# Windowed attention in front of a mixture of experts: scores of each chunk of queries with its own keys only, and a softmax that reads the banks

## The chip, the cores and the metric

One core of one Trainium2 chip. The time is that of one execution on the device, in microseconds (us). PE is TensorE, DVE VectorE, ACT ScalarE, POOL GpSimd, and SP the queue that issues all the DMAs. A "bank" is a part of PSUM, the memory that TensorE writes; the other tiles lie in SBUF.

## The reference

Attention over chunks of 32 queries: a chunk sees 16 keys to its left, its own 32 and 8 to its right (fewer at the ends of the sequence), and 8 memory keys, 64 in all. There are 4 batches, 8 heads, 768 positions and a head size of 64. The result goes through 4 experts, each weighted by a probability of the token.

```python
for c in range(nc):                        # 24 chunks of 32
    q_c = q[:, :, c_start:c_end]
    k_full = np.concatenate([mem_k, k[:, :, l_start:r_end]], axis=2)
    v_full = np.concatenate([mem_v, v[:, :, l_start:r_end]], axis=2)
    scores = scale * np.matmul(q_c, k_full.transpose(0, 1, 3, 2))
    scores = scores - np.max(scores, axis=-1, keepdims=True)
    a = np.exp(scores)
    a = a / (np.sum(a, axis=-1, keepdims=True) + 1e-09)
    out[:, :, c_start:c_end] = np.matmul(a, v_full)
...
for e in range(E):                         # x: 3072 x 512
    h = np.maximum(x @ w1[e], 0.0)         # 512 x 1024
    out += p[:, e:e + 1] * (h @ w2[e])     # 1024 x 512
```

## The kernel before

The work of the attention is cut into 32 units of 96 queries, three chunks (`UQ` = 96, `NCU` = 3): eight units a batch, four batches. A unit has a window of 128 keys, the 120 that its three chunks see and the 8 memory keys put in at column 56 (`MEM`). TensorE multiplies all 96 queries with all 128 keys, head by head. The heads go in pairs: head size 64 fills half of TensorE's rows, and the two heads of a pair (`j` = 0, 1) lie in the two halves. Their scores go to the two banks of one tile (`s_ps`, or `att_ps` in the head).

Of each row of 128 scores a chunk needs 64 (`KW`). `PIECES` says which: 0 to 64 for the first chunk, 32 to 96 for the second, and for the third the memory's 8 at column 56 and 56 from column 72. Four copies for a unit bring them into `s_sb` (96 x 8 x 64, a `spot` in the head for most units), where keys outside of the sequence are filled with a very low number. Maximum, exponential, sum and division run on `s_sb`. Four more copies spread the result over `band` (96 x 8 x 128), which is zero elsewhere, and `band` is turned into `aT` (128 keys by 96 queries): in seven 32x32 block transposes on VectorE in the steady part, on TensorE in the head. TensorE multiplies `aT` with the values into `x_ps`. The attention's output is the experts' input `x`.

There are three stages. In the **head**, `early_scores`, `early_turn` and `early_mix` work on the eight units of the first batch (S, T and X in the text `FIRST_BLOCK`), among them products of the first expert (M, N) and products of zeros (W). In the steady part the experts of one batch run while `window` works on the next batch's units: nine calls of it for a batch, each of which scores one unit and then mixes the unit before. The experts' products make up nearly all of TensorE's work.

The order on TensorE is that in which the program adds its steps. The order on the other engines, and for some steps the engine, is drawn by a planner (`Plan`): it tries random changes against costs written by hand (`t_act`, `t_dve`, `pe(1.0, ...)`), and keeps the best. So any change of the steps draws the order of all others anew. `act`, `dve`, `moved` and `join` each add a step: on ScalarE, on VectorE, on either of these two, and on VectorE or GpSimd. The profile puts their instructions on the helper's line (L528 copies, L541 and L542 `moved`, L546 and L547 `join`).

The lines that matter: L588 and L1300 the scores, L607 and L1391 the mix with the values, L1372 the transposes on TensorE in the head, L640 and L1326 the maximum, L643 the exponentials, L660 the transposes on VectorE.

Of the kernel before, what the change touches and what calls it, by code (L numbers as in the profile page):

```python
# [13 lines left out]
AF = mybir.ActivationFunctionType  # L14
# [382 lines left out]

MEM = W
PIECES = [[(0, KW, 0)], [(0, KW, CH)], [(0, NM, MEM), (NM, KW, 2 * CH + NM)]]

# [14 lines left out]
def tile_chunked_attention_moe(ctx: ExitStack, tc: tile.TileContext, qk, v, probs, w1, w2, out):  # L415
# [58 lines left out]
    def real(t, c):  # L474

        return LC if t == 0 and c == 0 else 0, KW - RC if t == NU - 1 and c == NCU - 1 else KW
# [45 lines left out]
    def pe(time, fn, reads, writes):  # L522
        now["plan"].add("PE", time, fn, reads, writes)
# [44 lines left out]
    def want_qk(u):  # L568

        width = NPAIR * (UQ + P)  # L570
        t = late_st.setdefault(u, {})["qk"] = new(
            lambda: late["sb"], [P, width + (40 if "fin" in late else 0)], "qk_t", 1)
        dma(lambda: t.ap[:, 0:width], lambda: qk[u], P * width * 4, [], [t])

    def window(us, i, last=False):

        band, aT = bands[0], aTs[0]
        if i < len(us):
            u = us[i]
            want_v(u)  # L580
            s_ps = new(lambda: late["s"], [P, H, P], "s_ps", 1)
            qk_t = late_st[u]["qk"]

            def scored():
                for g in range(NPAIR):
                    for j in range(2):
                        rows = slice(j * D, (j + 1) * D)
                        nc.tensor.matmul(  # L588
                            s_ps.ap[0:UQ, j * NPAIR + g, :],
                            lhsT=qk_t.ap[rows, g * UQ:(g + 1) * UQ],  # L590
                            rhs=qk_t.ap[rows, NPAIR * UQ + g * P:NPAIR * UQ + (g + 1) * P],
                            start=True, stop=True,
                        )
# [26 lines left out]
        s_sb = new(lambda: att, [UQ, H, KW], "s_sb", 2, parts=NCU + H)  # L620
        mx, sm = (new(lambda: att, [UQ, H, 1], name, 2, parts=k) for name, k in (("mx", 1), ("sm", H)))

        def fill(rows, cols, part):
            now["plan"].add("POOL", 0.2, lambda: nc.gpsimd.memset(s_sb.ap[rows, :, cols], LOWEST), [], [(s_sb, part)])

        def take(rows, dst, src, cols, part):
            act(lambda: s_sb.ap[rows, :, dst], lambda: s_ps.ap[rows, :, src], cols, [s_ps], [(s_sb, part)], psum=True)

        for c in range(NCU):
            rows = slice(c * CH, (c + 1) * CH)  # L630
            first, end = real(t, c)
            if first:
                fill(rows, slice(0, first), c)
            if end < KW:
                fill(rows, slice(end, KW), c)
            for lo, hi, at in PIECES[c]:
                a, b = max(lo, first), min(hi, end)
                take(rows, slice(a, b), slice(at + a - lo, at + b - lo), (b - a) * H, c)
        n_s = H * KW
        dve(lambda: nc.vector.tensor_reduce(out=mx.ap[:, :, 0], in_=s_sb.ap, axis=AX.X, op=ALU.max), n_s, [s_sb], [mx])  # L640
        act(lambda: mx.ap, lambda: mx.ap, H, [], [mx], func=AF.Copy, scale=-scale)
        for h in range(H):
            now["plan"].add("ACT", t_act(KW) + 0.01, lambda h=h: nc.scalar.activation(  # L643
                s_sb.ap[:, h, :], s_sb.ap[:, h, :], AF.Exp, bias=mx.ap[:, h, :], scale=scale, accum_out=sm.ap[:, h, :],
            ), [mx, s_sb], [(s_sb, NCU + h), (sm, h)])
# [6 lines left out]
        join(lambda: s_sb.ap, lambda: s_sb.ap, lambda: sm.ap.broadcast_to([UQ, H, KW]), ALU.mult, n_s, [sm], [s_sb])  # L652
        for c in range(NCU):
            rows = slice(c * CH, (c + 1) * CH)
            for lo, hi, at in PIECES[c]:
                act(lambda rows=rows, lo=lo, hi=hi, at=at: band[rows, :, at:at + hi - lo],
                    lambda rows=rows, lo=lo, hi=hi: s_sb.ap[rows, :, lo:hi], (hi - lo) * H, [s_sb], [("band", c)])
        for c in range(NCU):
            for kb in sorted({k // CH for lo, hi, at in PIECES[c] for k in range(at, at + hi - lo)}):
                dve(lambda c=c, kb=kb: nc.vector.transpose(  # L660
                        out=aT[kb * CH:(kb + 1) * CH, :, c * CH:(c + 1) * CH],
                        in_=band[c * CH:(c + 1) * CH, :, kb * CH:(kb + 1) * CH]),
                    268, [("band", c)], [("aT", c)])
# [622 lines left out]
    def early_scores(u):  # L1286
        b, t = units[u]
        if u % 2 == 0:
            first["pair"] = new(lambda: head, [P, H * (UQ + P)], "qk_pair", 2, parts=2)
        pair, i = first["pair"], u % 2  # L1290
        width = NPAIR * (UQ + P)
# [3 lines left out]
        def scored():  # L1295
            x = pair.ap[:, i * width:(i + 1) * width]
            for g in range(NPAIR):
                for j in range(2):
                    rows = slice(j * D, (j + 1) * D)
                    nc.tensor.matmul(  # L1300
                        s_ps.ap[0:UQ, j * NPAIR + g, :],
                        lhsT=x[rows, g * UQ:(g + 1) * UQ], rhs=x[rows, NPAIR * UQ + g * P:NPAIR * UQ + (g + 1) * P],
                        start=True, stop=True,
                    )

        pe(1.1, scored, [(pair, i)], [s_ps])
# [4 lines left out]
        for c in range(NCU):  # L1311
            rows = slice(c * CH, (c + 1) * CH)
            begin, end = real(t, c)
            for cols in ((0, begin), (end, KW)):
                if cols[0] < cols[1]:
                    now["plan"].add("POOL", 0.2, lambda rows=rows, cols=slice(*cols): nc.gpsimd.memset(
                        s.ap[rows, :, cols], LOWEST), [], [(s, c)])
            for lo, hi, at in PIECES[c]:
                a, z = max(lo, begin), min(hi, end)
                moved(lambda rows=rows, a=a, z=z: s.ap[rows, :, a:z],  # L1320
                      lambda rows=rows, a=at + a - lo, z=at + z - lo: s_ps.ap[rows, :, a:z],
                      (z - a) * H, [s_ps], [(s, c)])
# [3 lines left out]
        dve(lambda: nc.vector.tensor_reduce(out=mx.ap[:, :, 0], in_=s.ap, axis=AX.X, op=ALU.max), n_s, [s], [mx])  # L1326
        dve(lambda: nc.vector.tensor_tensor(
            out=s.ap, in0=s.ap, in1=mx.ap.broadcast_to([UQ, H, KW]), op=ALU.subtract), n_s, [mx], [s], two=True)
# [281 lines left out]
def _layout(q, k, v, mem_k, mem_v, moe_domain_probs, moe_w1, moe_w2):  # L1610
    def windows(m, x):
        pad = np.pad(x, ((0, 0), (0, 0), (LC, RC), (0, 0)))
        cuts = (t * UQ for t in range(NU))
        return np.stack(
            [np.concatenate([pad[:, :, a:a + MEM], m, pad[:, :, a + MEM:a + LC + UQ + RC]], axis=2) for a in cuts], axis=1
        )

    qT = q.reshape(B, NPAIR, 2, NU, UQ, D).transpose(0, 3, 2, 5, 1, 4)
    kT = windows(mem_k, k).reshape(B, NU, NPAIR, 2, P, D).transpose(0, 1, 3, 5, 2, 4)
    U = B * NU  # L1620
    qk = np.concatenate([qT.reshape(U, P, -1), kT.reshape(U, P, -1)], axis=2)
    vw = windows(mem_v, v).transpose(0, 1, 3, 2, 4).reshape(B, NU, P, H * D)
# [26 lines left out]
```

## Time and profile before

| | |
|---|---|
| median of 3 runs | 1057.07 us (1056.67 to 1060.95) |
| the profiled execution | 1057.3 us, its span 1055.5 us |
| busy: PE, DVE, ACT, POOL | 99%, 76%, 60%, 46% of the span |
| granted clock of TensorE, mean | 0.998 |
| DMA | 300.23 MB, 284 GB/s over the span |

The span goes from the first to the last instruction; the rest of the execution's time lies around it. An engine counts as busy while it has an instruction under way; matmuls overlap, so a busy TensorE can still have room.

### The profile page before, as it was taken

The numbers are of one execution on the slowest core, as the hardware profiler recorded it, in microseconds if no ns is written. First come the engines' busy times: TensorE is split into PE (matmuls) and PEld (weight loads), VectorE is DVE, ScalarE is ACT, GpSimd is POOL, SyncE is SP. The second block draws the span as 40 slices with busy tenths as digits, with TensorE's granted clock in tenths as the row PEclk, the third lists the DMA queues.
The fourth block names the chain that finished last, engine by engine and source line by source line (L and its number), as shares of the span: only waits on it lengthen the run. The fifth ranks groups of instructions, "written<-read, shape, count | busy, mean of one in ns | idle before, by whom it ended". The sixth has DMA issues, their size and how long they took to land.

```text
span 1055.5 us, 19540 instructions
## 1 busy us (share of the span) xinstructions
PE 1042.1 (99%) x6875; PEld 998.5 (95%) x6875; DVE 804.2 (76%) x1339; ACT 632.0 (60%) x1599; POOL 486.5 (46%) x448
## 2 busy tenths in 40 slices
PE   7999999999999999999999999999999999999998
PEld 6988988989989999999999999999999999999998
DVE  6858787967986767668798967969689875939485
ACT  6837886767847867585865666556573534334241
POOL 3537564644614546173252715336062644626170
PEclk9999999999999999999999999999999999999999
DMA  8557899989979999899888888879779887878774
GB/s 271 190 191 255 317 349 341 384 309 345 352 278 387 331 327 300 303 347 323 307 260 287 267 269 275 278 241 292 241 237 287 296 263 244 268 243 277 246 251 150
DMA packets 185505, 300.23 MB, mean 284 GB/s; under 512 B 14816, under 2 KB 125504, under 8 KB 185408
## 3 DMA queue, kind: packets, MB, share of 16 engines
q1 hardware_dynamic: 185408, 298.99, 83.9%
q8 instruction: 55, 0.90, 0.4%
q14 instruction: 42, 0.34, 0.1%
HBM read 229.69 MB, written 69.26 MB: 283 GB/s over the span
## 4 chain that ended last, share of the span: by engine, by line
PE 91%; DVE 5%; ACT 1%; DMA 1%; issue 1%; SPq 0%; POOL 0%; DVEq 0%; ACTq 0%
PE a_ps L884 22%; PE moe_ps L884 16%; PE a_ps L1168 12%; PE moe_ps L864 12%; PE moe_ps L1168 9%; PE a_ps L1124 7%; PE moe_ps L1124 5%; PE moe_ps L818 3%; PE s_ps L588 2%; PE x_ps L607 2%; DVE A_lo L546 2%; DVE u L984 1%; DVE u L546 1%; PE x_ps L1391 1%; DMA raw_pair<-in_w_dram 0%
## 5 line engine op out<-in xcount | busy, mean ns | idle before, releaser
L547 POOL TENSOR_TENSOR u<-u,routes 128x384 f32<-128x384 f32 x44 | 47.8, 1086 | 191.8 <-ACT u L530 191.8
L546 DVE TENSOR_TENSOR A_lo<-u,A_hi 128x384 fp32r<-128x384 f32 x133 | 116.8, 893 | 13.9 <-ACT A_hi L528 13.5
L864 PE MATMUL moe_ps<-w,h_hi 128*128 128x512 f32 x384 | 119.8, 393 | 0.0
L546 DVE TENSOR_TENSOR u<-moe_ps,u 128x384 f32<-128x384 f32 x120 | 66.3, 553 | 65.5 <-PE moe_ps L884 50.5
L528 ACT COPY u<-a_ps 128x384 f32<-128x384 f32 x120 | 57.1, 476 | 67.5 <-PE a_ps L884 66.4
L528 ACT CAST A_hi<-u 128x384 fp32r<-128x384 f32 x144 | 72.7, 513 | 31.0 <-DVE u L984 25.6
L547 POOL TENSOR_TENSOR raw<-raw 128x256 f32<-128x256 f32 x62 | 57.3, 925 | 72.9 <-DMA raw<-in_w_dram 69.6
L547 POOL TENSOR_TENSOR us<-u,u 128x384 f32<-128x384 f32 x48 | 55.7, 1160 | 66.5 <-ACT u L530 31.2
L864 PEld LDWEIGHTS moe_ps<-w,h_hi 128*128 128x128 f32 x384 | 71.2, 188 | 14.8
L884 PE MATMUL a_ps<-xc_hi,ring 128*128 128x384 f32 x384 | 82.5, 337 | 0.1
L530 ACT ACTIVATE u<-u 128x384 f32<-128x384 f32 x96 | 50.1, 524 | 48.3 <-DVE u L546 47.8
L660 DVE STREAM_TRANSPOSE aT<-band 32x256 f32<-32x256 f32 x168 | 73.0, 435 | 6.0 <-ACT band L528 3.1
L864 PE MATMUL moe_ps<-w,h_lo 128*128 128x512 f32 x192 | 75.0, 391 | 0.0
L884 PEld LDWEIGHTS a_ps<-xc_hi,ring 128*128 128x128 f32 x384 | 67.8, 188 | 0.5 <-ACT u L528 0.4
L1168 PE MATMUL a_ps<-A_hi,ring 128*128 128x384 f32 x256 | 65.5, 337 | 1.0 <-DVE u L984 1.0
L643 ACT ACTIVATE s_sb<-s_sb,mx 96x64 f32<-96x64 f32 x192 | 64.4, 337 | 0.7
L547 POOL TENSOR_TENSOR u<-u,us 128x384 f32<-128x384 f32 x46 | 57.7, 1256 | 6.0 <-ACT A_hi L528 2.8
L547 POOL TENSOR_TENSOR u<-u,u 128x384 f32<-128x384 f32 x46 | 59.3, 1289 | 0.5
L528 ACT COPY band<-s_sb 32x512 f32<-32x512 f32 (+2 forms) x100 | 48.9, 510 | 13.7 <-DVE s_sb L546 9.4
L528 ACT COPY s_sb<-s_ps 32x64 f32<-32x64 f32 (+2 forms) x96 | 44.7, 466 | 20.4 <-PE s_ps L588 19.3
L547 POOL TENSOR_TENSOR us<-u,us 128x384 f32<-128x384 f32 x45 | 51.9, 1153 | 4.6 <-DVE Sb_lo L546 1.5
L547 POOL TENSOR_TENSOR w<-raw,w 128x512 fp32r<-128x512 f32 x23 | 33.3, 1449 | 39.1 <-ACT w L528 35.7
(241 smaller groups left out, 3179.2 us busy)
## 6 DMA issues: line engine op xcount, KB each, us to landing
ring<-k SPq DMA_DIRECT2D x144, 512.0 KB, 4.8
ring<-t SPq DMA_DIRECT2D x96, 512.0 KB, 5.6
ring<-w SPq DMA_DIRECT2D x72, 512.0 KB, 5.4
k<-w SPq DMA_DIRECT2D x48, 512.0 KB, 5.0
w<-w SPq DMA_DIRECT2D x32, 512.0 KB, 5.4
raw<-in_w_dram SPq DMA_DIRECT2D x62, 256.0 KB, 5.0
ring<-k SPq DMA_DIRECT2D x48, 256.0 KB, 4.5
qk_t<-in_qk_dram SPq DMA_DIRECT2D x24, 448.0 KB, 6.2
```

What stands on the lines that cost most here:

```text
L528: nc.scalar.copy(out(), x())
L530: nc.scalar.activation(out(), x(), func)
L546: ("DVE", t_dve(cols), lambda: nc.vector.tensor_tensor(out=out(), in0=x(), in1=y(), op=op)),
L547: ("POOL", t_pool(cols), lambda: nc.gpsimd.tensor_tensor(out=out(), in0=x(), in1=y(), op=op)),
L588: nc.tensor.matmul(s_ps.ap[0:UQ, j * NPAIR + g, :], lhsT=qk_t.ap[rows, g * UQ:(g + 1) * UQ], rhs=qk_t.ap[rows, NPAIR * UQ + g * P:NPAIR * ...
L643: now["plan"].add("ACT", t_act(KW) + 0.01, lambda h=h: nc.scalar.activation(s_sb.ap[:, h, :], s_sb.ap[:, h, :], AF.Exp, bias=mx.ap[:, h, : ...
L660: dve(lambda c=c, kb=kb: nc.vector.transpose(out=aT[kb * CH:(kb + 1) * CH, :, c * CH:(c + 1) * CH], in_=band[c * CH:(c + 1) * CH, :, kb * ...
L818: nc.tensor.matmul(ps.ap[:, lo:hi], lhsT=a[:, c * P:(c + 1) * P], rhs=x[:, c, lo:hi], start=(i == 0), stop=(i == len(steps) - 1),)
L864: nc.tensor.matmul(self.ps.ap, lhsT=h.ap[:, self.rows], rhs=w.ap[:, part, :], start=(i == 0 and k == 0), stop=(i == NF - 1 and k == 2),)
L884: nc.tensor.matmul(ps.ap[:, 0:SG], lhsT=a()[:, c * P:(c + 1) * P], rhs=y[:, k0 + c, :], start=(first and i == 0), stop=(i == len(steps) - ...
L1124: nc.tensor.matmul(ps.ap[:, cols], lhsT=x.ap[:, rows], rhs=w_ap[:, y, :], start=(begins and k == 0 and i == 0), stop=(k == NP2 - 1 and i = ...
L1168: nc.tensor.matmul(ps.ap[:, 0:SG], lhsT=w_ap[:, y, rows], rhs=x.ap, start=(begins and k == 0 and i == 0), stop=(k == NP2 - 1 and i == 2), ...
```

## The change

The scores of a chunk are made with its own 64 keys alone: 24 products a unit (4 pairs, 3 chunks, 2 heads) in place of 8. Each has 32 queries, put at the chunk's 32 partitions of the bank, and so lies in one of three strips of 32 columns of TensorE and one of its two row halves. The third chunk finds its keys side by side because the memory keys are laid out a second time, behind the window: 136 keys for a unit (`KEYS`) in place of 128, its loads 928 columns wide in place of 896.

The four copies out of the bank are left out. The maximum, the exponentials (in the head the subtraction) and nothing else read the bank. Keys outside of the sequence are overwritten in the bank, by VectorE in place of GpSimd. In `window` only the third chunk still goes through `band`; the first two are transposed from `s_sb`, since their keys lie at multiples of 32. The head keeps its `band`.

```diff
-PIECES = [[(0, KW, 0)], [(0, KW, CH)], [(0, NM, MEM), (NM, KW, 2 * CH + NM)]]
+KEYS = P + NM
+STARTS = (0, CH, 2 * CH + NM)
+PIECES = [[(0, KW, 0)], [(0, KW, CH)], [(0, KW - NM, 2 * CH + NM), (KW - NM, KW, MEM)]]
...
+    def scores(s_ps, x):
+        def fn():
+            for g in range(NPAIR):
+                for c in range(NCU):
+                    for j in range(2):
+                        rows = slice(j * D, (j + 1) * D)
+                        k0 = NPAIR * UQ + g * KEYS + STARTS[c]
+                        nc.tensor.matmul(
+                            s_ps.ap[c * CH:(c + 1) * CH, j * NPAIR + g, 0:KW],
+                            lhsT=x()[rows, g * UQ + c * CH:g * UQ + (c + 1) * CH], rhs=x()[rows, k0:k0 + KW],
+                            start=True, stop=True,
+                        )
+        return fn
+    def outside(t, s_ps):
+        for c, edge, cols in ((0, 0, slice(0, LC)), (NCU - 1, NU - 1, slice(KW - NM - RC, KW - NM))):
+            if t == edge:
+                dve(lambda c=c, cols=cols: nc.vector.memset(s_ps.ap[c * CH:(c + 1) * CH, :, cols], LOWEST),
+                    (cols.stop - cols.start) * H, [], [s_ps])
...
     def window(us, i, last=False):
-            pe(1.0, scored, [qk_t], [s_ps])
+            pe(1.0, scores(s_ps, lambda: qk_t.ap), [qk_t], [s_ps])
...
-        for c in range(NCU):
-            for lo, hi, at in PIECES[c]:
-                take(rows, slice(a, b), slice(at + a - lo, at + b - lo), (b - a) * H, c)
+        s_in = lambda: s_ps.ap[0:UQ, :, 0:KW]
+        outside(t, s_ps)
-        dve(... tensor_reduce(out=mx.ap[:, :, 0], in_=s_sb.ap, ... op=ALU.max), n_s, [s_sb], [mx])
+        dve(... tensor_reduce(out=mx.ap[:, :, 0], in_=s_in(), ... op=ALU.max), n_s, [s_ps], [mx])
-                s_sb.ap[:, h, :], s_sb.ap[:, h, :], AF.Exp, bias=mx.ap[:, h, :], scale=scale, accum_out=sm.ap[:, h, :],
+                s_sb.ap[:, h, :], s_in()[:, h, :], AF.Exp, bias=mx.ap[:, h, :], scale=scale, accum_out=sm.ap[:, h, :],
...
+        rows = slice(2 * CH, UQ)
+        for lo, hi, at in PIECES[2]:
+            act(... band[rows, :, at:at + hi - lo] ... s_sb.ap[rows, :, lo:hi] ...)
         for c in range(NCU):
-            for lo, hi, at in PIECES[c]:
-                act(... band[rows, :, at:at + hi - lo] ... s_sb.ap[rows, :, lo:hi] ...)
...
+            for kb in ((0, 1), (1, 2), (1, 2, 3))[c]:
+                if c < 2:
+                    x = lambda rows=rows, k=kb - c: s_sb.ap[rows, :, k * CH:(k + 1) * CH]
+                else:
+                    x = lambda rows=rows, kb=kb: band[rows, :, kb * CH:(kb + 1) * CH]
+                dve(lambda x=x, kb=kb, rows=rows: nc.vector.transpose(out=aT[kb * CH:(kb + 1) * CH, :, rows], in_=x()),
+                    268, [s_sb if c < 2 else ("band", 2)], [("aT", c)])
...
     def early_scores(u):
-        pe(1.1, scored, [(pair, i)], [s_ps])
+        pe(1.1, scores(s_ps, lambda: pair.ap[:, i * width:(i + 1) * width]), [(pair, i)], [s_ps])
+        s_in = lambda: s_ps.ap[0:UQ, :, 0:KW]
-                moved(... s.ap[rows, :, a:z] ... s_ps.ap[rows, :, a:z] ...)
+        outside(t, s_ps)
-        dve(... tensor_reduce(... in_=s.ap, ... op=ALU.max), n_s, [s], [mx])
+        dve(... tensor_reduce(... in_=s_in(), ... op=ALU.max), n_s, [s_ps], [mx])
-            out=s.ap, in0=s.ap, in1=mx.ap.broadcast_to([UQ, H, KW]), op=ALU.subtract), n_s, [mx], [s], two=True)
+            out=s.ap, in0=s_in(), in1=mx.ap.broadcast_to([UQ, H, KW]), op=ALU.subtract), n_s, [mx, s_ps], [s])
```

## Rows read from the trace of the kernel before

**Rows 1.** The page, parts 1 and 4: TensorE's busy time; the chain by engine.

```profile
PE 1042.1 (99%) x6875; PEld 998.5 (95%) x6875; DVE 804.2 (76%) x1339; ACT 632.0 (60%) x1599; POOL 486.5 (46%) x448
...
PE 91%; DVE 5%; ACT 1%; DMA 1%; issue 1%; SPq 0%; POOL 0%; DVEq 0%; ACTq 0%
```

**Rows 2.** Windows: the stretch and its length, each engine's busy us, clock, DMA.

```profile
10.00:20.00 10.00, 6.44 (x83) 5.75 (x80) 8.90 (x17) 8.73 (x17) 1.73 (x2) 0.86 0.98 281
20.00:30.00 10.00, 8.90 (x112) 8.10 (x110) 7.91 (x14) 8.64 (x19) 5.52 (x5) 0.96 0.70 237
30.00:40.00 10.00, 10.00 (x104) 9.30 (x103) 9.21 (x21) 9.12 (x21) 6.16 (x6) 1.00 0.50 142
...
100.00:400.00 300.00, 300.00 (x1879) 274.96 (x1879) 229.16 (x382) 215.90 (x571) 152.21 (x150) 1.00 0.93 337
```

**Rows 3.** TensorE's waits: us in total, times, longest.

```profile
PE att_ps L1372 <- issue: 2.8, 1, 2.8
...
PE att_ps L1300 <- DVE s_sb L542: 1.1, 1, 1.1
...
PE x_ps L1391 <- ACT aT L541: 0.8, 1, 0.8
PE x_ps L1391 <- ACT spot L532: 0.8, 1, 0.8
PE att_ps L1300 <- ACT s_sb L541: 0.6, 1, 0.6
PE att_ps L1372 <- ACT band L528: 0.3, 1, 0.3
```

**Rows 4.** The tile of scores, steady part: duration ns min/median/max, first and last start, forms.

```profile
L588 PE MATMUL s_ps<-qk_t x384: 268/269/348, 86.3 to 761.2; 64*96 64x128 f32 x192
L528 ACT COPY s_sb<-s_ps x96: 203/526/581, 87.4 to 763.1; 32x512 f32<-32x512 f32 x45, 32x64 f32<-32x64 f32 x24, 32x448 f32<-32x448 f32 x21, 32x384 f32<-32x384 f32 x6
```

**Rows 5.** The chain at 31 us and from 104 to 127: start, us, what.

```profile
31.05 0.66 PE att_ps L1372 x8
...
104.73 1.05 PE s_ps L588 x16
105.78 0.81 PE x_ps L607 x16
...
124.80 1.05 PE s_ps L588 x16
```

**Rows 6.** TensorE's timeline, cut off at 86.27 and at 86.50 us.

```profile
86.25 0.35 PE L588 MATMUL s_ps<-qk_t 64*96 64x128 f32 x2
...
86.25 0.46 PE L588 MATMUL s_ps<-qk_t 64*96 64x128 f32 x4
```

**Rows 7.** Timeline of ScalarE and VectorE, 104.4 to 127: one unit's softmax.

```profile
105.83 1.92 ACT L528 COPY s_sb<-s_ps 32x64 f32<-32x64 f32 x4 [0.37 <-PE s_ps L588]
...
111.52 0.33 ACT L643 ACTIVATE s_sb<-s_sb,mx 96x64 f32<-96x64 f32 x1
...
114.60 1.26 ACT L528 COPY band<-s_sb 32x512 f32<-32x512 f32 x2
...
115.90 1.34 DVE L660 STREAM_TRANSPOSE aT<-band 32x256 f32<-32x256 f32 x3 [0.21 <-ACT band L528]
```

**Rows 8.** The page, part 6: the loads of queries and keys.

```profile
qk_t<-in_qk_dram SPq DMA_DIRECT2D x24, 448.0 KB, 6.2
```

**Rows 9.** Groups by line and form, 0 to 35 us, VectorE.

```profile
L1399 DVE TENSOR_TENSOR xa_lo<-x_ps,xa_hi 128x384 fp32r<-128x384 f32 x4 | 2.2, 555 | 2.4 <-ACT aT L541 1.5 <-PE x_ps L1271 0.5 <-ACT xa_hi L528 0.4
L1326 DVE TENSOR_REDUCE mx<-spot 96x8 f32<-96x512 f32 x3 | 2.0, 678 | 0.1
...
L1327 DVE TENSOR_TENSOR spot<-spot,mx 96x512 f32<-96x512 f32 x2 | 1.4, 688 | 0.1
```

**Rows 10.** The tile of scores in the head: one of its four groups of copies.

```profile
L541 ACT COPY spot<-att_ps x21: 195/561/578, 10.4 to 54.3; 32x512 f32<-32x512 f32 x11, 32x448 f32<-32x448 f32 x5, 32x64 f32<-32x64 f32 x4, 32x384 f32<-32x384 f32 x1
```

**Rows 11.** The chain from 4 to 36 us: the last copy of the first unit.

```profile
6.87 0.63 DVE s_sb L542
```

More of the change, by code (lines that the diff above doesn't have):

```diff
@@ L582, in window @@
             qk_t = late_st[u]["qk"]
[L584 to L593, printed above, removed]
-            pe(1.0, scored, [qk_t], [s_ps])
+            pe(1.0, scores(s_ps, lambda: qk_t.ap), [qk_t], [s_ps])
             if not last and u + 1 < len(units):
@@ L619, in window @@
         b, t = units[u]
-        s_sb = new(lambda: att, [UQ, H, KW], "s_sb", 2, parts=NCU + H)
+        s_sb = new(lambda: att, [UQ, H, KW], "s_sb", 2, parts=H)
         mx, sm = (new(lambda: att, [UQ, H, 1], name, 2, parts=k) for name, k in (("mx", 1), ("sm", H)))
[L623 to L627, printed above, removed]
-        for c in range(NCU):
[L630 to L635, printed above, removed]
-            for lo, hi, at in PIECES[c]:
-                a, b = max(lo, first), min(hi, end)
-                take(rows, slice(a, b), slice(at + a - lo, at + b - lo), (b - a) * H, c)
+        s_in = lambda: s_ps.ap[0:UQ, :, 0:KW]
+        outside(t, s_ps)
         n_s = H * KW
-        dve(lambda: nc.vector.tensor_reduce(out=mx.ap[:, :, 0], in_=s_sb.ap, axis=AX.X, op=ALU.max), n_s, [s_sb], [mx])
+        dve(lambda: nc.vector.tensor_reduce(out=mx.ap[:, :, 0], in_=s_in(), axis=AX.X, op=ALU.max), n_s, [s_ps], [mx])
         act(lambda: mx.ap, lambda: mx.ap, H, [], [mx], func=AF.Copy, scale=-scale)
         for h in range(H):
-            now["plan"].add("ACT", t_act(KW) + 0.01, lambda h=h: nc.scalar.activation(
-                s_sb.ap[:, h, :], s_sb.ap[:, h, :], AF.Exp, bias=mx.ap[:, h, :], scale=scale, accum_out=sm.ap[:, h, :],
-            ), [mx, s_sb], [(s_sb, NCU + h), (sm, h)])
+            now["plan"].add("ACT", t_act(KW) + 0.08, lambda h=h: nc.scalar.activation(
+                s_sb.ap[:, h, :], s_in()[:, h, :], AF.Exp, bias=mx.ap[:, h, :], scale=scale, accum_out=sm.ap[:, h, :],
+            ), [mx, s_ps], [(s_sb, h), (sm, h)])
         def inverted():
@@ L652, in window @@
         join(lambda: s_sb.ap, lambda: s_sb.ap, lambda: sm.ap.broadcast_to([UQ, H, KW]), ALU.mult, n_s, [sm], [s_sb])
+        rows = slice(2 * CH, UQ)
+        for lo, hi, at in PIECES[2]:
+            act(lambda lo=lo, hi=hi, at=at: band[rows, :, at:at + hi - lo], lambda lo=lo, hi=hi: s_sb.ap[rows, :, lo:hi],
+                (hi - lo) * H, [s_sb], [("band", 2)])
         for c in range(NCU):
             rows = slice(c * CH, (c + 1) * CH)
-            for lo, hi, at in PIECES[c]:
[L656 to L663, printed above, removed]
+            for kb in ((0, 1), (1, 2), (1, 2, 3))[c]:
[5 more added lines that the diff above has]
+                    268, [s_sb if c < 2 else ("band", 2)], [("aT", c)])
     def combine_x(first):
@@ L1288, in early_scores @@
         if u % 2 == 0:
-            first["pair"] = new(lambda: head, [P, H * (UQ + P)], "qk_pair", 2, parts=2)
+            first["pair"] = new(lambda: head, [P, H * (UQ + KEYS)], "qk_pair", 2, parts=2)
         pair, i = first["pair"], u % 2
-        width = NPAIR * (UQ + P)
+        width = NPAIR * (UQ + KEYS)
         dma(lambda: pair.ap[:, i * width:(i + 1) * width], lambda: qk[u], P * width * 4, [], [(pair, i)])
         s_ps = new(lambda: ps_head, [P, H, P], "att_ps", 2)
[L1295 to L1304, printed above, removed]
-        pe(1.1, scored, [(pair, i)], [s_ps])
+        pe(1.1, scores(s_ps, lambda: pair.ap[:, i * width:(i + 1) * width]), [(pair, i)], [s_ps])
+        s_in = lambda: s_ps.ap[0:UQ, :, 0:KW]
         if u < 2:
@@ L1310, in early_scores @@
             s = now["plan"].slot("s_spot", s_spots, NCU)
[L1311 to L1322, printed above, removed]
+        outside(t, s_ps)
         mx, sm = (new(lambda: head, [UQ, H, 1], name, NU) for name in ("mx0", "sm0"))
```

20 lines of the change are left out of this document (9 added, 11 removed).

## The prediction

> **What bounds the kernel now.** I read the page first: TensorE is busy 99% of the span and the chain of work that ended last lies 91% on it [rows 1]. The table by stage says where this holds: from 100 to 400 us (and the two rows behind it, to 1000, are alike) TensorE is busy throughout, while VectorE and ScalarE are busy for some three quarters of the time. The exception is the head, where TensorE was busy 6.4 of the 10 us from 10 to 20 and ran at a mean granted clock of 0.86 there [rows 2]. The list of TensorE's waits puts numbers to it: 6.4 us in six waits, all for the attention's softmax of the first units (2.8 + 1.1 + 0.8 + 0.8 + 0.6 + 0.3) [rows 3]; the list's other entries name no tile that the change touches. So there are two prices. A microsecond of TensorE work added or removed in the steady part is a microsecond of the result. A microsecond of ScalarE or VectorE counts in the head alone.
>
> **TensorE: the scores.** Per unit the change replaces 8 products (96 queries by 128 keys) by 24 (32 queries by 64 keys), for 24 units in `window` and 8 in `early_scores`. Each product leaves two matmul records (384 for 24 x 8 products [rows 4]), so 16 records become 48, each with half the columns. Whether this costs or gives depends on how many of them run beside each other.
>
> What the trace shows of that: eight records of the head's transposes, 96 columns each, which use the whole width one after another, take 0.66 us on the chain, 82 ns each. The 16 records of 96 columns that mix the values, in two column halves of the array, take 0.81 us, where one after another they would take 16 x 82 = 1.31. The scores' 16 records of 128 columns, in two row halves, take 1.05 [rows 5]. So both kinds of halves work side by side, in 8 steps of two. A close cut shows the same: two score records start in the first 0.02 us, and only four have started after 0.25 [rows 6]. Since the first two start together although the program issues both records of a product before the next product, the halves advance independently.
>
> The step grows with the columns: (1.05 - 0.81) / 8 = 30 ns for 32 more columns [rows 5]. For 64 columns, eight steps therefore take 0.81 - 0.24 = 0.57 us, and a step, from the transposes' 82 less 27 to 30, is some 55 ns. The new products lie in two row halves times three column strips of 32, six places. The kernel's order goes through all six before it returns to one. If all six work side by side, 48 records are 8 steps: 0.57 us, and I add 0.03 for the four more starts: **0.60 us instead of 1.05, a gain of 0.45 a unit.** No row shows three strips at once, nor row halves and strips together, so this is bounded: from below by these 8 steps, from above by no overlap at all, 48 x 0.055 + 0.13 of ends (0.57 less 8 x 0.055) = 2.77 us. I take six, because each kind of split is shown by rows of its own to run its parts beside each other; the values' two strips even share one bank, as the three strips of a row half will.
>
> Units that count: 24 in `window`, and in the head the first, whose scores begin the chain of the softmax, and the last three, which fall after 30 us, when TensorE is no longer idle [rows 2]: 28 x 0.45 = **-12.6 us**. The four others fall among the waits and belong to the head, below.
>
> The Trainium skill has a rule against this change. "TensorE: Matmul & The Clock Gate", section "Wait — 56ns, not 53.3ns?", says that from start to start of matmuls it never goes below about 25 ns, however small they are. In the close cut two starts are nearer than that, but as one pair in different halves; as an average over a block no row refutes the rule. As an estimate from its figure, 48 records would take 1.2 us plus ends, and the change would lose.
>
> **ScalarE, VectorE, GpSimd in the steady part.** Removed per unit: four copies out of the bank (1.92 us on ScalarE) and two of the four band copies (1.26 us). Maximum and exponentials read the bank instead. A bank read isn't dearer: ScalarE's copies of 32x512 take 0.53 us from the bank [rows 4], not more than the 0.63 each of the two band copies [rows 7], and VectorE's 0.56 for 384 columns from a bank lies on the line of its 0.68 for 512 from SBUF [rows 9]. The seven transposes stay. I count all of this as nothing: the unit whose scores ran at 104.73 had its last transpose done at 117.24 and was wanted at 125.85, behind the next scores of 124.80, 8.6 us later [rows 5, 7], and no such wait stands in TensorE's list [rows 3]. With that cover gone the 3.2 us would be a gain, not a loss, so nothing is at risk here. The two edge memsets a batch move from GpSimd to VectorE: 8 small ones.
>
> The bank of scores is now held until the last exponential instead of the last copy: until about 111.85 instead of 107.75 in that unit, and the next scores come at 124.80 [rows 5, 7]. That leaves 13 us to spare. It stands before the mix in TensorE's order, and the mix already needs the same unit's transposes, which end later than its exponentials: it can't end last.
>
> **DMA.** The unit's queries and keys grow from 448 to 464 KB (896 to 928 columns), 32 times. They are issued one unit ahead and land in 6.2 us at the median [rows 8], against the 20 us between the two score blocks of [rows 5]. The same number of issues stand in the same places of SP's queue: nothing.
>
> **The head.** Here 32 copies from the bank go away, four for each of eight units, most of them on ScalarE (21 in one group, at a median of 0.56) [rows 10]: about 16 us of ScalarE and VectorE at 0.5 each. Those of the first unit lie on the chain, the last until 7.50 [rows 11], before its maximum can begin. In exchange a bank is held until maximum and subtraction are through (0.68 + 0.69 us [rows 9]), with two banks for the units. At most the 6.4 us of waits and some 1.8 us lost to the lower clock (0.14 and 0.04 of 10 us each) could come back. But the words of the first block still set the units' order by hand, the loads of values and weights come at their own times, and the order is drawn again by the planner. I take a third of the 8 us, **-2.5 us**, with bounds of -8 and +2; the lower one lets every wait vanish, the upper one prices three of these bank waits at 0.7 each.
>
> **Sum.** Against the profiled execution (1057.3 us, 1.8 outside its span; the median of the runs is 1057.07): 1057.3 - 12.6 - 2.5 = **1042.2 us**.
>
> **Rivals.**
>
> *Three side by side* (strips and row halves don't combine): 16 steps, 0.57 + 8 x 0.055 + 0.03 = 1.04 us, as now. Only the head remains: 1054.8. For it: no row shows more than two. Against: the halves' independence.
>
> *An issue limit.* The places are free, but TensorE can't start records as fast as they come free. Six places ask for one record every 9 ns (0.055 / 6). The rows show two in 0.02 us, 10 ns each, for one pair [rows 6], and over a whole block no more than 16 in 0.81 us, 51 ns each [rows 5]. Taken about halfway between, in ratio, at 25 ns: 48 x 25 = 1.2 us, plus 0.13: 1.33, +0.28 a unit, +7.8 over 28, with the head 1062.6, slower. For it: nothing faster than 51 ns over a block was seen. Against: the paired starts. (The page of the Trainium skill named above has a limit of this size.) The block's 1.05 us decides the sign: more than 19 ns a record and the change loses on TensorE.
>
> *Two side by side*, as in every block of the trace: 24 steps, 0.60 + 16 x 0.055 = 1.48 us, +0.43 a unit, +12.0: 1066.8. For it: the same count of two in both kinds of split. (One at a time, 2.77 us, would be +48 us; the halves rule it out.) Against: each is a split into two, so two is all that could be seen.
>
> *The head gives nothing or loses.* The bank waits replace the copies: 1057.3 - 12.6 + 2 = 1046.7.
>
> **Chances and range.** Six places 0.56, the head rival 0.08, three 0.15, the issue limit 0.11, two or fewer 0.10. The predicted time is that of the first. From 1036 (six places, the whole 8 us of the head) to 1064 (the issue limit, with room of 1.4 us) the range leaves out the two-wide case and part of the limit. The likeliest case alone gives 1036 to 1047. A difference under 0.5%, 5.3 us, can't be told from none: faster 0.64 (six places and the head rival), same 0.15 (three), slower 0.21 (the other two).
>
> **What would show it.** Right: the score block on the chain at 0.55 to 0.65 us with 48 records, some six starts in its first 0.06 us; TensorE's busy time down by 10 to 15 us; ScalarE's copies and band copies down by some 76 us over the 24 units (24 x 3.18); the waits of the head shorter. Wrong: a block over 1.05 us; starts in twos; a wait of the scores on an exponential in TensorE's list; or a head in which the waits of [rows 3] stay.

## The result, and the profile after

The changed kernel takes 1044.36 us (median of 4 runs, 1043.5 to 1045.35), the kernel before, timed beside it, 1059.01 (4 runs, 1056.67 to 1063.24). The ratio is 0.9858, 95% interval 0.982 to 0.9895: faster by 1.0 to 1.8%. The profiled execution took 1043.5 us with a span of 1041.7; predicted were 1042.2, in a range of 1036 to 1064.

The page, parts 1, 4 and 6, of the kernel after:

```profile
PE 1030.7 (99%) x7899; PEld 988.8 (95%) x7899; DVE 809.4 (78%) x1358; ACT 539.3 (52%) x1426; POOL 464.9 (45%) x426
...
PE 93%; DVE 4%; DMA 1%; issue 1%; POOL 0%; ACT 0%; SPq 0%; DVEq 0%; POOLq 0%; ACTq 0%
...
qk_t<-in_qk_dram SPq DMA_DIRECT2D x24, 464.0 KB, 6.3
```

Beside [rows 1], TensorE lost 11.4 us of busy time though it has 1024 more matmul records, and the chain lies on it a little more than before. ScalarE lost 92.7 us, close to the 76 + 16 that the copies were priced at. In the steady part that could not shorten anything: from 100 to 1000 us TensorE waited for ScalarE neither before nor after. The longer load still lands in 6.3 us [rows 8].

The tile of scores in the steady part (duration in ns min/median/max, first and last start, forms):

```profile
L485 PE MATMUL s_ps<-qk_t x1152: 216/216/241, 82.9 to 748.1; 64*32 64x64 f32 x192
...
L639 ACT ACTIVATE s_sb<-s_ps,mx x192: 292/309/328, 85.3 to 752.6; 96x64 f32<-96x64 f32 x192
...
L636 DVE TENSOR_REDUCE mx<-s_ps x24: 669/676/689, 84.4 to 748.6; 96x8 f32<-96x512 f32 x24
```

The maximum out of the bank takes 676 ns at the median, where the same form took 678 out of SBUF in the head before [rows 9]; the exponentials out of the bank take 309 ns, one out of SBUF took 0.33 us before [rows 7]. A bank read is not dearer.

One record's 216 ns is latency, not cost. The cost is on the chain of the kernel after (start, us, what):

```profile
82.98 0.67 PE s_ps L485 x46
...
101.01 0.67 PE s_ps L485 x46
101.67 0.81 PE x_ps L618 x16
```

A block of scores takes 0.67 us, where [rows 5] had 1.05 (46 of the 48 records are in the chain's count). The mix of the values beside it stayed at 0.81. How the records overlap is seen where TensorE's timeline is cut off, first at 101.00, then at 101.05 us:

```profile
100.94 0.27 PE L485 MATMUL s_ps<-qk_t 64*32 64x64 f32 x6
...
100.94 0.32 PE L485 MATMUL s_ps<-qk_t 64*32 64x64 f32 x11
```

Six records had started 0.06 us after the first, eleven after 0.11. [rows 6] had two and, a quarter of a microsecond later, four. So six records start together, as many as there are places.

The head, 10 to 40 us, and one steady stretch, by stage (columns as in [rows 2]):

```profile
10.00:20.00 10.00, 7.64 (x115) 6.89 (x101) 7.43 (x13) 6.27 (x14) 1.51 (x1) 0.70 0.94 273
20.00:30.00 10.00, 8.40 (x139) 7.55 (x136) 8.67 (x17) 8.74 (x21) 5.37 (x4) 1.00 0.76 274
30.00:40.00 10.00, 9.92 (x167) 9.35 (x168) 9.79 (x19) 8.01 (x18) 5.23 (x5) 1.00 0.81 293
...
100.00:400.00 300.00, 299.96 (x2264) 275.99 (x2263) 229.07 (x393) 188.28 (x535) 151.16 (x148) 1.00 0.95 345
```

The steady stretch is as full of TensorE as before. From 10 to 20 us TensorE is busier than in [rows 2], but at a granted clock of 0.70 instead of 0.86: part of that busy time is slower work (from 10 to 15.9 us it ran at 0.50, the lower of the clock's two levels). What it waited for there (us in total, times, longest):

```profile
PE att_ps L485 <- DMA qk_pair<-in_qk_dram: 1.8, 1, 1.8
PE att_ps L485 <- issue: 1.7, 1, 1.7
PE x_ps L1369 <- ACT aT L563: 1.4, 2, 0.8
...
PE att_ps L1350 <- ACT band L550: 0.6, 1, 0.6
PE att_ps L1350 <- POOL band L569: 0.3, 1, 0.3
```

That is 5.8 us beside the 6.4 of [rows 3], and the two longest are new: the scores wait for their own load, and the scores of the fourth unit stop for 1.7 us for nothing that the profile shows.

**Where the 13.8 us of span come from.** The first steady block of scores starts on the chain at 82.98 us, before at 86.32: 3.3 us, of which the three late blocks of the head give 3 x 0.38 = 1.1 and the rest of the head 2.2 (1.8 without the first unit's block, which the prediction counted with the others). Of these, 1.2 us are one wait of the kernel before, from 80.7 to 81.9 us, that the kernel after doesn't have (a row of the list of TensorE's waits before, as in [rows 3]):

```profile
PE moe_ps L818 <- DVE h_lo L804: 1.2, 1, 1.2
```

It is a wait of an expert's product for VectorE, which the chain traces back to a load of weights; the change touches none of these tiles. Before has it under another draw too (1.4 us), after under neither (experiment 3); why it went is not shown. That leaves some 0.6 us of the 1.8 for all else in the head, the softmax's waits of [rows 3] among it.

From the first steady block to the end of the span it is 958.7 us, before 969.2: 10.5, of which 24 blocks give 24 x 0.38 = 9.1. The last 1.4 belong to no step of the change that I can name; the experiments show how large such remainders get.

### The profile page after: what moved, and what is told of

Same layout as the page of the kernel before. It is cut to its first block, busy times and chain, and to the rows that moved or that the text cites. A ratio compares the mean times of both kernels' runs of the same rounds, so it can differ in the third digit from the quotient of the medians.

```text
span 1041.7 us, 21404 instructions
## 1 busy us (share of the span) xinstructions
PE 1030.7 (99%) x7899; PEld 988.8 (95%) x7899; DVE 809.4 (78%) x1358; ACT 539.3 (52%) x1426; POOL 464.9 (45%) x426
## 4 chain that ended last, share of the span: by engine, by line
PE 93%; DVE 4%; DMA 1%; issue 1%; POOL 0%; ACT 0%; SPq 0%; DVEq 0%; POOLq 0%; ACTq 0%
PE a_ps L883 22%; PE moe_ps L883 16%; PE moe_ps L863 13%; PE a_ps L1167 12%; PE moe_ps L1167 10%; PE a_ps L1123 7%; PE moe_ps L1123 5%; PE moe_ps L817 3%; PE x_ps L618 2%; PE s_ps L485 2%; DVE A_lo L568 1%; DVE u L983 1%; DVE u L568 1%; DMA raw<-in_w_dram 1%; DMA qk_pair<-in_qk_dram 1%
## 5 line engine op out<-in xcount | busy, mean ns | idle before, releaser
L569 POOL TENSOR_TENSOR u<-u,routes 128x384 f32<-128x384 f32 x46 | 50.3, 1095 | 191.8 <-ACT u L552 191.5
L569 POOL TENSOR_TENSOR raw<-raw 128x256 f32<-128x256 f32 x57 | 51.2, 899 | 127.1 <-DMA raw<-in_w_dram 83.1
L569 POOL TENSOR_TENSOR us<-u,u 128x384 f32<-128x384 f32 x43 | 49.4, 1149 | 41.8 <-DVE u L983 20.3
L569 POOL TENSOR_TENSOR us<-u,us 128x384 f32<-128x384 f32 x43 | 49.5, 1151 | 30.2 <-DVE us L568 23.7
L639 ACT ACTIVATE s_sb<-s_ps,mx 96x64 f32<-96x64 f32 x192 | 57.1, 309 | 0.7
L568 DVE TENSOR_TENSOR acc<-a_ps,acc 128x384 f32<-128x384 f32 x52 | 28.8, 553 | 26.7 <-PE a_ps L1167 26.1
L883 PE MATMUL a_ps<-xc_lo,ring 128*128 128x384 f32 x192 | 48.9, 336 | 0.0
L1167 PEld LDWEIGHTS a_ps<-A_hi,ring 128*128 128x128 f32 x256 | 45.8, 188 | 2.4 <-DVE u L983 2.2
L569 POOL TENSOR_TENSOR w<-raw,w 128x512 fp32r<-128x512 f32 x25 | 35.9, 1443 | 26.7 <-ACT w L550 17.6
```

Source lines behind the costliest of these rows:

```text
L568: ("DVE", t_dve(cols), lambda: nc.vector.tensor_tensor(out=out(), in0=x(), in1=y(), op=op)),
L569: ("POOL", t_pool(cols), lambda: nc.gpsimd.tensor_tensor(out=out(), in0=x(), in1=y(), op=op)),
L639: now["plan"].add("ACT", t_act(KW) + 0.08, lambda h=h: nc.scalar.activation(s_sb.ap[:, h, :], s_in()[:, h, :], AF.Exp, bias=mx.ap[:, h, :] ...
L883: nc.tensor.matmul(ps.ap[:, 0:SG], lhsT=a()[:, c * P:(c + 1) * P], rhs=y[:, k0 + c, :], start=(first and i == 0), stop=(i == len(steps) - ...
L1167: nc.tensor.matmul(ps.ap[:, 0:SG], lhsT=w_ap[:, y, rows], rhs=x.ap, start=(begins and k == 0 and i == 0), stop=(k == NP2 - 1 and i == 2), ...
```

## The experiments

**The theory**: TensorE's gain comes from six places that work side by side, for 10 to 11 us; the head gives some 2 more. **Rivals**: the gain is the softmax's, through a ScalarE that is relieved (then the products alone give nothing); the places are fed at a limited rate and 0.67 is that limit; the difference is what a new draw of the planner's order gives (then the same edit under another draw loses it).

### 1. The small products alone

The new products and their columns stay; the softmax is that of before, with its copies out of the bank and all band copies. The core of the edit, against the changed kernel:

```diff
-        s_in = lambda: s_ps.ap[0:UQ, :, 0:KW]
-        outside(t, s_ps)
+            has, lacks = parts_at(t, c)
+            for a, b in lacks:
+                fill(rows, slice(a, b), c)
+            for a, b in has:
+                take(rows, slice(a, b), slice(a, b), (b - a) * H, c)
```

> The 24 small products alone; the four copies out of the bank, the GpSimd memsets, the softmax on the copy and all band copies stay as before. Theory (the gain lies on TensorE): score block 0.67 us as in the changed kernel, 28 blocks on the path give back 28 x 0.38 = 10.6 us, so 1046 to 1050 us where before measures 1059. Rival (the gain lies in the copies taken off ScalarE and VectorE): the block is short too, but the time stays within 3 us of before.

Measured: 1053.24 us, ratio 0.9946 (0.9932 to 0.9961), so -5.9 us and not the -10 that the theory asked for. The block is 0.67 us as in the whole change. From 100 to 1000 us its waits are

```profile
PE a_ps L891 <- DVE u L567: 1.6, 3, 0.7
PE a_ps L891 <- DMA ring<-k: 1.4, 2, 1.0
PE a_ps L1175 <- DVE u L991: 1.1, 1, 1.1
PE a_ps L891 <- ACT u L549: 0.5, 2, 0.3
```

and those of the kernel after in the same stretch

```profile
PE a_ps L1167 <- DVE u L983: 0.3, 1, 0.3
```

So the blocks saved 24 x 0.38 = 9.1 us, and 4.6 us of waits (before has 0.7 in that stretch), of products that the change does not touch, took a good part of it. Whether that belongs to the old softmax or to the draw, experiment 3 asks.

### 2. The new softmax alone

Maximum and exponentials read the bank and two chunks are turned without a band; the products are the old eight of 96 by 128. Against the changed kernel:

```diff
             for g in range(NPAIR):
-                for c in range(NCU):
-                    for j in range(2):
+                for j in range(2):
...
-                            s_ps.ap[c * CH:(c + 1) * CH, j * NPAIR + g, 0:KW],
+                        s_ps.ap[0:UQ, j * NPAIR + g, :],
```

> The other half: the softmax reads the banks and two chunks turn without a band, but the scores are made as before, 8 products of 96 queries by 128 keys (the second and third chunk then read the first 64 columns, other keys than their own, so this times the work and not the result). Theory: block 1.05 us; only what the head and single waits gave stays, 1053 to 1057 us. Rival: 1044 to 1047 us, nearly the whole gain.

Measured: 1052.98 us, ratio 0.9945 (0.9933 to 0.9957): -6.1. The steady part gave nothing: from its first block (81.5) to the end of the span (1050.9) it is 969.4 us, before 969.2. All of it came in the head, which is 4.7 us shorter. Its first transposes in TensorE's timeline:

```profile
12.30 0.85 PE L1349 MATMUL att_ps<-ident,band 96*128 96x96 f32 x8 [0.76 <-ACT band L549]
```

In the trace of before they start at 15.41, where the longest wait of [rows 3] ends. The profile calls that wait "issue", but the chain shows ScalarE's last copy into `band` ending at 15.31, just ahead of it (first the chain, then TensorE's timeline):

```profile
15.07 0.24 ACT band L528
...
15.41 0.85 PE L1372 MATMUL att_ps<-ident,band 96*128 96x96 f32 x8 [2.77 <-issue]
```

In the kernel after they start at 15.79 (experiment 6). So the copies were on the head's path, and their removal is worth more there than I took (3.5 us, without the 1.2 us wait of the expert's product, which is gone here as well); but the whole change does not keep it.

### 3. Another draw of the planner's order

The order in which instructions of the later stages are issued is drawn from a seed. The same kernels with another one:

```diff
-        plan.run(ahead=LEAD)
+        plan.run(seed=2, ahead=LEAD)
...
-        plan.run(last=True)
+        plan.run(seed=2, last=True)
```

Before:

> The kernel before with another seed for the planner's draws of the two stages behind the head; nothing else. It shows what a new draw alone is worth. If draws hardly matter: within 2 us of before (1057 to 1061). If they do: off by 3 to 6 us, most of it as waits of TensorE between 100 and 1000 us.

The products alone:

> The small products alone (copies and old softmax kept) with the other seed. The first draw gave 1053.2, with 4.6 us of waits of TensorE on VectorE, ScalarE and a load between 100 and 1000 us that before doesn't have. If those are the luck of the draw: they go, and the time is 1046 to 1050. If the copies, which fill ScalarE, cause them: they stay, 1052 to 1055.

After:

> The changed kernel with the other seed. If the draw is luck alone: within some 4 us of 1044 to either side. If the relief of ScalarE makes the draw robust: within 1.5 us of 1044.

Measured, in one series against a common run of before (1060.18): before 1062.29 (ratio 1.0028, 1.0012 to 1.0043), the products alone 1049.87 (0.9914, 0.9893 to 0.9935), after 1045.59 (0.9868, 0.985 to 0.9886). The draw is worth 1 to 2 us in the whole kernels and 3.4 in the products alone. Under this draw the products alone are 12.4 us faster than before, under the first 5.9; their blocks give 10.6 in both. Their waits from 100 to 1000 us did not go, as they should have if the first draw alone had made them: 2.8 us are left of the 4.6, and before has 3.0 us under this draw instead of 0.7. The rival of a lucky draw falls: after is faster under both, by 14.7 and 16.7 us.

### 4. The order of the 24 products

In the change the loops are head pair, chunk, row half. Once the chunk is outermost (all products of one column strip first), once the row half:

```diff
-            for g in range(NPAIR):
-                for c in range(NCU):
+            for c in range(NCU):
+                for g in range(NPAIR):
                     for j in range(2):
```
```diff
-            for g in range(NPAIR):
-                for c in range(NCU):
-                    for j in range(2):
+            for j in range(2):
+                for g in range(NPAIR):
+                    for c in range(NCU):
```

Chunk outermost:

> The changed kernel with the loop over chunks outermost: all products of one column strip come before those of the next, so that neighbours in the program share two places instead of six. If TensorE sends records to whatever place is free from far ahead in its queue, the block stays near 0.67 us and the time at 1044. If only neighbours overlap, 24 steps of two: a block of about 1.48 us and 1044 + 28 x 0.81 = 1067 us. If it looks ahead by part of a block: in between.

Row half outermost:

> The changed kernel with the row half outermost: neighbours use three column strips of one half. Free look-ahead: 0.67 us and 1044 us. Neighbours only: 16 steps of three, about 1.04 us and 1044 + 28 x 0.37 = 1054 us. It also shows whether three strips of one half run beside each other at all, which no row of before showed.

Measured, one run each: 1055.04 and 1048.87 us. The block of scores, on the chain of the kernel with the chunk outermost:

```profile
145.40 1.09 PE s_ps L485 x48
```

and with the row half outermost:

```profile
144.96 0.84 PE s_ps L485 x47
```

TensorE's timeline of the first, cut off 0.02 us after the block began, shows

```profile
145.33 0.25 PE L485 MATMUL s_ps<-qk_t 64*32 64x64 f32 x2
```

and of the second, 0.03 us after,

```profile
144.89 0.25 PE L485 MATMUL s_ps<-qk_t 64*32 64x64 f32 x3
```

They start in twos and in threes, the number of places that the first products in program order reach. That pairs follow each other faster than every 56 ns is ruled out by a later cut of the first, at 0.24 us:

```profile
145.33 0.41 PE L485 MATMUL s_ps<-qk_t 64*32 64x64 f32 x8
```

Eight had started, where 24 equal steps, (1.09 - 0.22) / 24 = 36 ns each, would have brought fourteen; so more than two must run at once later in the block. If TensorE saw the whole block ahead, both orders would take 0.67 us; if it saw neighbours alone, twos would take 1.48 and threes 1.04, by the sums of the two rivals. Both blocks lie between: TensorE passes over records that wait for a place, but not over the whole block. The order of the loops alone is worth 0.42 us a block. The times follow: against after they are 10.7 and 4.5 us longer, and 28 blocks of 0.42 and 0.17 us more would make 11.8 and 4.8.

### 5. The products made twice

```diff
             pe(1.0, scores(s_ps, lambda: qk_t.ap), [qk_t], [s_ps])
+            pe(1.0, scores(s_ps, lambda: qk_t.ap), [qk_t], [s_ps])
```

> The changed kernel with the 24 products of each of the 24 steady units made twice, the second time over the first. If a second set streams in six places, it adds 8 steps of 0.056 = 0.45 us a unit, a block of 1.12 and 10.8 us in all. If the sequencer's supply of instructions binds once its full queue is used up, as the starts in the second half of a block (11 to 17 ns apart) suggest, it adds 48 x 0.0145 = 0.70, a block of 1.37 and 16.7 us.

Measured, one run: 1059.92 us. The double block, on the chain:

```profile
121.27 1.12 PE s_ps L485 x93
```

The second 48 records add 0.45 us, 8 steps of 56 ns: the step of the prediction (55), and 9.4 ns a record. The 14 ns a record of a single block are therefore no rate limit; its 0.67 us are 0.45 of steps and 0.22 of ends. (A limit at 9.4 ns itself could not be told from six places of 56 ns each.) The Trainium skill's rule of about 25 ns from start to start, which the prediction weighed ("TensorE: Matmul & The Clock Gate", section "Wait — 56ns, not 53.3ns?"), does not hold across places: as an estimate from its figure, the second set would have added 1.2 us. The time rose by 15.6 us where 24 x 0.45 = 10.8 were added; the rest to the span's end, less its blocks, is 5.9 us longer than that of after (table below), with 3.9 us of waits from 100 to 1000 us where after has 0.3. I put that down to the new draw; no run of this edit under a fixed plan shows it.

### 6. Fewer zeros ahead of the transposes

The hand-written order of the head issues products of zeros ("W" and a number of them) to keep TensorE going. The fourth unit's scores are S3, and the stall of 1.7 us lies inside them. Either the 30 zeros behind S3 become 8, or the 32 ahead of S0 become 12, or both:

```diff
-W32 S0 S1 S2 W6 S3 W30 T0 ...
+W32 S0 S1 S2 W6 S3 W8 T0 ...
```
```diff
-W32 S0 S1 S2 W6 S3 W30 T0 ...
+W12 S0 S1 S2 W6 S3 W30 T0 ...
```
```diff
-W32 S0 S1 S2 W6 S3 W30 T0 ...
+W12 S0 S1 S2 W6 S3 W8 T0 ...
```

W30 to W8:

> The changed kernel with 8 zero products in place of 30 behind the head's fourth score block. They took 3.3 us on the chain there, at the low clock. Theory (they and the stall before them hold back the first transpose): it comes at 13 to 13.6 us instead of 15.8, and the first score block of the steady part 1 to 2.5 us earlier than 82.9. Rival (the weight loads bind the rest of the head, or fewer zeros keep the clock low for longer): that block stays within 0.7 us of 82.9. The stall inside the fourth block stays where it is, behind 222 matmul records.

W32 to W12:

> The changed kernel with 12 zero products in place of 32 at its very start. If the 1.7 us stall inside the fourth score block is TensorE waiting for its next instructions, it depends on how many were used up, not on what they do: 20 records fewer ahead, so it moves 20 records on, past the end of that block into the zero products behind it (8 records of the block and 12 zeros later). If it is something of that block (its bank, its load), it stays inside it.

Both:

> Both: 12 zeros at the start and 8 behind the fourth score block. Theory: that block runs through, no stall falls ahead of the first transpose, which comes at 12.3 to 13 us, and the first score block of the steady part at 80.5 to 82: 1041 to 1043.5 us in all, a little better than the changed kernel. Rival (loads or clock bind the head): within 1 us of 1044.4.

Measured: 1049.93, 1046.33 (one run each) and 1048.43 us (ratio 0.9903, 0.9883 to 0.9922). None beats the change, although the first steady block of scores came early in all three, at 81.1, 80.9 and 81.4 us, and the transposes too (12.60, 12.95, 12.34): what was won in the head was lost behind it (table below). First, TensorE's timeline of the kernel after:

```profile
8.31 0.71 PE L485 MATMUL att_ps<-qk_pair 64*32 64x64 f32 x48 [1.84 <-DMA qk_pair<-in_qk_dram]
...
9.48 1.07 PE L485 MATMUL att_ps<-qk_pair 64*32 64x64 f32 x40
12.24 0.44 PE L485 MATMUL att_ps<-qk_pair 64*32 64x64 f32 x8 [1.69 <-issue]
12.61 3.38 PE L1270 MATMUL x_ps<-idle 128*128 128x128 bf16 x30
15.79 0.97 PE L1350 MATMUL att_ps<-ident,band 96*128 96x96 f32 x8
```

then of W30 to W8:

```profile
8.78 0.65 PE L485 MATMUL att_ps<-qk_pair 64*32 64x64 f32 x40 [0.16 <-issue]
11.77 0.32 PE L485 MATMUL att_ps<-qk_pair 64*32 64x64 f32 x8 [2.34 <-issue]
```

and of W32 to W12:

```profile
9.19 1.09 PE L485 MATMUL att_ps<-qk_pair 64*32 64x64 f32 x48
10.22 0.84 PE L1270 MATMUL x_ps<-idle 128*128 128x128 bf16 x12
11.95 1.17 PE L1270 MATMUL x_ps<-idle 128*128 128x128 bf16 x18 [0.88 <-issue]
```

After: 32 zeros, 144 score records, 6 zeros, 40 score records, stall: 222 records. W8 changes what comes later, and the stall stays at 222. W12 takes 20 records from the front, and the stall moves 20 records on, out of S3 into the zeros: 12 + 144 + 6 + 48 + 12 = 222. The six other kernels with the small products and 32 zeros (experiments 1, 3, 4 and 5) stop behind their 222nd record as well, for 0.7 to 2.1 us. It begins after the same number of records, whichever these are, so it hangs on no tile; that fits an engine that has used up the instructions it has and waits for the next. The queue table of the kernel after, 9.6 to 10.9 us (packets, MB, share), shows one packet of instructions among 275 of data that fill the engines:

```profile
q1 hardware_dynamic: 275, 0.50, 100.0%
q8 instruction: 1, 0.02, 4.8%
```

In all nine kernels that stop, the stall ends 2.3 to 2.5 us after such a packet starts, and moves with it: the packet starts at 8.9 us and the stall ends at 11.34 in the products alone under the other draw, 9.95 and 12.44 in after under that draw. So the two go together; that the packet holds the instructions TensorE lacks is likely, but not shown. Before and in experiment 2, S0 to S3 are 64 records and not 192, and neither trace has a stall among them.

### 7. Fewer zeros under the same plan

An edit of the order makes the planner draw all that follows again. Here it still counts 32 and 30 zeros, but at most 12 are issued:

```diff
-            for _ in range(n):
+            for _ in range(min(n, 12)):
```

> The changed kernel with 12 zero products at each of the two long places of the head (32 and 30 before), while the planner still counts the old numbers: so every other engine has the same order of work as the changed kernel, in all stages. If the losses of the three runs with fewer zeros came from new draws of the later stages: the first score block of the steady part comes at 80.5 to 82 us instead of 82.9, what follows it takes 958 to 960 us as in the changed kernel, and the time is 1041 to 1043.5 us. If fewer zeros cost something themselves: that block comes no earlier, or the rest takes 962 us or more.

Measured: 1044.31 us, ratio 0.9866 (0.9842 to 0.9889), the same as the change. The timeline has the transposes early, held up by ScalarE's band copy and no longer by TensorE's own work:

```profile
12.21 0.85 PE L1350 MATMUL att_ps<-ident,band 96*128 96x96 f32 x8 [0.84 <-ACT band L550]
```

but the windows have a low granted clock in two stretches:

```profile
10.00:20.00 10.00, 7.33 (x92) 6.37 (x82) 8.08 (x16) 8.17 (x17) 1.51 (x1) 0.71 0.87 245
20.00:30.00 10.00, 9.71 (x134) 8.92 (x130) 7.79 (x17) 7.20 (x16) 5.11 (x4) 0.78 0.78 283
```

and the waits end at the same place as in the kernel after, with a GpSimd band product just ahead of 30.35 us (after: 30.08):

```profile
PE att_ps L1350 <- POOL band L569: 0.6, 1, 0.6
```

The 3.6 us won at the first transposes were gone 18 us later. Most of them went to the clock: from 14 to 24 us it was granted at 0.50 to 0.52, and in TensorE's timeline the two mixes, the second transposes, the scores and the zeros of that stretch take 7.2 us, where after they take 4.2. Why the clock fell is not shown; idle time alone does not explain it, since W32 to W12 has less of TensorE's time busy from 10 to 20 us (6.88 against 7.33) at a clock of 1.00. After itself has its low stretch earlier, and its chain then lies on a load of weights:

```profile
19.78 7.96 DMA raw<-in_w_dram
```

From its first steady block (83.2) to the end this kernel takes 958.9 us, as after. So fewer zeros by themselves cost the steady part nothing, and what the three kernels of experiment 6 lost there is best put down to the new draw: from 100 to 1000 us they have 4.3, 3.5 and 5.8 us of waits, this one and after 0.3. The 1.5 to 2 us that their heads won may be the new draw's too, since under the old plan they do not come.

### All kernels by the same cut

Start of the first steady block of scores, end of the span, and the stretch between them less its 24 blocks, in us:

| kernel | first block | span | between | block | between less 24 blocks |
|---|---|---|---|---|---|
| before / other draw | 86.3 / 87.9 | 1055.5 / 1061.0 | 969.2 / 973.1 | 1.05 | 944 / 948 |
| products alone / other draw | 84.2 / 83.0 | 1051.2 / 1046.8 | 967.0 / 963.8 | 0.67 | 951 / 948 |
| softmax alone | 81.5 | 1050.9 | 969.4 | 1.05 | 944 |
| after / other draw | 82.9 / 82.9 | 1041.7 / 1044.1 | 958.8 / 961.2 | 0.67 | 943 / 945 |
| chunk / row half outermost | 83.9 / 84.2 | 1053.3 / 1047.1 | 969.4 / 962.9 | 1.09 / 0.84 | 943 / 943 |
| products twice | 82.6 | 1058.1 | 975.5 | 1.12 | 949 |
| W8 / W12 / both | 81.1 / 80.9 / 81.4 | 1048.2 / 1044.6 / 1051.7 | 967.1 / 963.7 / 970.3 | 0.67 | 951 / 948 / 954 |
| 12 zeros, same plan | 83.2 | 1042.1 | 958.9 | 0.67 | 943 |

The last column should be one number if the blocks were all that differed. It goes from 943 to 954; of the three at 950 and more, two have a reordered head. But each value is one execution, and executions of one kernel differ by 2 to 7 us: that of "both" is the slowest of its six, 5 us above their median, that of after the fastest of its four. Differences of 2 or 3 us in this column therefore say little. The four kernels that keep the old copies average 947.8, the six with the new softmax and the head's order unchanged (without the run under the same plan) 944.5. That may be some 3 us from a relieved ScalarE, the draw, or the spread of single executions; so few of them don't settle it.

## Why the prediction was right, point by point

**Six places side by side**: right, shown by the starts in sixes, by the blocks of experiment 4 that fall back to twos and threes when the order does, and by the 0.45 us of a second set. Three, two, and the issue limit fall: the block is 0.67 us, with 14 ns a record, under the 19 from which the change would have lost.

**The size of a block**: the step of 55 ns was right (56). The term that was mis-sized is the ends: I had put them at 0.60 - 8 x 0.055 = 0.16 us, and they are 0.22. So the block lies just outside the 0.55 to 0.65 us that I had named as the sign of being right. The gain a block is 0.38 instead of 0.45, and 28 x 0.38 = 10.6 us instead of 12.6. TensorE's busy time, -11.4, says the same, since it also has the four other blocks of the head: 32 x 0.38 = 12.2, less the head's slower work (the 30 zeros alone take 1.5 us more).

**Nothing in the steady part from ScalarE, VectorE, GpSimd and the loads**: right within what the draw allows. The softmax alone left the steady part at 969.4 against 969.2 us. The exponentials do not hold the next scores up: no such wait stands in the list of after.

**The head, -2.5**: the size was nearly right (-1.8), the way to it not, so this was luck. I had expected the waits of [rows 3] to shrink; they became others of nearly the same sum, 5.8 us, close to what I had named as a sign of being wrong. And 1.2 of the 1.8 us are the expert's wait for `h_lo`, one of the entries of the list that I had set aside because the change touches none of their tiles. The copies were on the path (softmax alone: first transposes 3.1 us earlier, steady part 4.7 us earlier). What I had not priced is the other half of the change there: four units of scores are 192 records instead of 64 among the first, TensorE stops for 1.7 us among them, and the 30 zeros behind take 3.38 us at a granted clock of 0.50 instead of 1.85 at 1.00. That goes with the small products, though not why: in the seven kernels that have them and these 30 zeros, the zeros take 3.2 to 3.4 us, in the three with the old products 1.85. The step that failed is that the small products cost the head only columns.

**The sum**: 12.6 + 2.5 were predicted, 10.6 + 1.8 came, and 1.4 of the steady part's remainder beside them: 13.8, so 1043.5 in the profiled execution against 1042.2. That the sum came so near is in part luck: the 1.4 us, and 1.2 of the 1.8, came by no step of the prediction. That the halves alone (-5.9 and -6.1) add up to 2.7 us less than the whole (-14.7) is within what a draw is worth (3.4 us in the products alone), and not settled beyond that.

## What to carry to other kernels

Small products that lie in different parts of the array cost together one step for as many of them as there are free places, if neighbours in program order go to different places; write the loops so that the innermost ones change the place. Where many small instructions stand at the start of a kernel, count them as a cost of their own. And where a planner redraws the order after any edit, compare under a second draw, or hold the plan fixed, before a few microseconds are put down to the edit.

## What the runs showed of the hardware that was not expected

- Six fp32 products of 64 rows by 32 columns start within some 0.06 us and go on in steps of 56 ns, 9.4 ns a record over a second set of 48.
- TensorE passes over records that wait for their place, but not over all: the same 24 products take 0.67, 0.84 or 1.09 us by their order alone.
- TensorE stalled for 0.7 to 2.3 us after the same 222 matmul records in nine kernels, while the DMA engines were full of data loads; each time the stall ended 2.3 to 2.5 us after an instruction packet had started.
